# Two slots of one expert run together in a kernel of attention, mixture of experts and GLU

## The chip, the cores and the metric

The kernel runs on one core of a Trainium2 chip. A core has five engines that run their own instruction streams in order and wait for each other by semaphores: TensorE (PE in the profile), VectorE (DVE), ScalarE (ACT), GpSimd (POOL) and SyncE (SP, which here only issues transfers and reads registers). The metric is the device time of one execution in microseconds (us), the time of the slowest core, which is the only one here.

## The reference

Causal attention with a decay bias for 4 batches of 8 heads (576 positions, 64 dimensions) gives 2304 rows `x` of 512 values. Each row goes to one of 8 experts, the one with the largest logit, and the result to a gated linear layer.

```python
def _moe_ref(x, modality_id, w_gate, modality_bias, w1, w2):
    logits = x @ w_gate + modality_bias[modality_id]
    e_idx = np.argmax(logits, axis=1)
    ...
    gate_w = probs[np.arange(N), e_idx]
    for e in range(E):
        mask = e_idx == e
        h = np.maximum(x[mask] @ w1[e], 0.0)
        out[mask] = gate_w[mask, None] * (h @ w2[e])
    return out

def _moe2_ref(x, w_gate, w_val, w_out):
    gate = 1.0 / (1.0 + np.exp(-(x @ w_gate)))
    val = x @ w_val
    return (gate * val @ w_out)
```

## The kernel before

The program is three stages on one hand-written order of instructions; every engine runs its instructions in the order in which the program issues them.

**Attention** works on 16 pairs of heads, four pairs to a batch, by a table of steps that repeats with each pair. Its PE work ends with `trx` and `ptx` (L381), which turn a pair's output into rows of x and its router logits (`lg`). DVE copies them to `xr` and `lg` (L404, L408).

**The router** works on a batch when its four pairs are through. `Router.batch` puts its steps on a list, and `tick`, called at fixed places of the attention's table, takes one of them and then leaves out `GAP[b]` calls; `SP[b]` calls are left out ahead of each scatter. The steps: a chain of ten short DVE instructions (L626 to L632, L655) finds the row's expert; two kinds of small matmuls, `rp` (L639, L641), give each row its rank among the rows of its expert; DVE turns that into an address, `r_ix` (L664); POOL scatters the row's number to a table in DRAM with five indirect DMAs (`tab`, L671); SP stores the rows themselves to `x` in DRAM (`rows_out`, L713). After batch 1 the expert with most rows so far is guessed, its first 512 row numbers are fetched (`idx0`), and SP loads the guessed expert's weights (`on_guess`): four chunks of w1 and w2, 512 KB each, into `raw`.

**The experts** run in slots of 256 rows. The first two slots (EARLY = 2) both belong to the guessed expert and take rows of batches 0 and 1; they start while batches 2 and 3 are still in the router. A slot needs its rows gathered (`gather`, two indirect DMAs on POOL, `xg`, L949), scaled by the gate (`gate`, L962, on POOL), and transposed on PE (`mtr`, L973, eight matmuls, then `xT` on ACT and DVE, L978 and L979). Its work is cut into eight pieces f of 128 hidden units. For each piece the fp32 weights are split into a high and a low part (`split`, tile `ew`: two casts on ACT at L922 and two subtractions on DVE at L925; the first three pieces do both on POOL, L920 and L925). One unit of PE work is `mm1` of a piece (12 matmuls, `ph`, L989) and then `mm2` of the unit before it (12 matmuls, L1009, into `sb` for an even slot, into `y` for an odd one). The 16 units of the first two slots are called u0 to u15 here; slot 0 is u0 to u7, slot 1 is u8 to u15, and each piece is split twice, once for each slot.

`look` (slot 0's transposes) and u0 stand inside the last steps of attention. Then `early` issues u1 to u15. Behind each unit it calls `main`, which takes up to 14 steps from the router's list (`pump`): batch 3's chain, its ranks and scatters, then `slots`, which computes the list of the remaining slots, fetches the 40 table rows that they need from `tab` into `tid` (POOL, L716, which waits until every scatter has landed) and transposes them on PE (`itr`, L725) into `idx`, the addresses for the gathers of slots 2 and on. In program order `itr` stands behind u7. Slot 2's weights are loaded into the same `raw` buffers when their old content has been split for slot 1. The results of a slot go through one buffer `yt` (L1021, two copies on ACT) to DRAM (L1023, SP).

Of the kernel before, what the change touches and what calls it, by code (L numbers as in the profile page):

```python
# [498 lines left out]
TROWS, PUMP = 96, 14  # L499
GAP, SP = [1, 1, 0, 0], [6, 3, 6, 0]  # L500
EARLY, EARLYB, MAIN, SLOTS, FIRST = 2, 2, 9, 14, 3
MAINH, HALVES, HROW, NROW = 2, 8, 32, 40


class Router:
# [102 lines left out]
    def batch(self, b, xr, lg):  # L608

        nc, cp, T = self.nc, self.cp, self.T  # L610
# [3 lines left out]
        tile_ = lambda shape, nm, dt=F32: cp.tile(shape, dt, tag="r_" + nm, name="r_" + nm)  # L614
        st = {}
        self.q.append(lambda: setattr(self, "gap", GAP[b]))
        bc = lambda a: a.unsqueeze(2).to_broadcast([128, 5, 8])
# [7 lines left out]
        q = self.q  # L625
# [42 lines left out]
        for t in range(5):  # L668
            rows = 64 if t == 4 else 128
            self.space(SP[b])  # L670
            q.append(lambda t=t, rows=rows: self.apart("tab", nc.gpsimd.indirect_dma_start(  # L671
                out=self.tab.rearrange("r c -> (r c)").unsqueeze(1),
                out_offset=bass.IndirectOffsetOnAxis(ap=ix[:rows, t : t + 1], axis=0),
                in_=self.ids[:rows, b, t : t + 1], in_offset=None, bounds_check=TROWS * 256 - 1, oob_is_err=True)))
            if t > 2:
                q.append(lambda t=t: self.rows_out(b, t, xr))
        if b == EARLYB - 1:
# [22 lines left out]
            q.append(lambda: V.tensor_copy(self.guess_i, gf[0:1]))  # L700
            q.append(self.on_guess)

    def rows_out(self, b, t, xr):

        x = self.x[2 * self.S * (b // 2) : 2 * self.S * (b // 2 + 1), :].rearrange("(p j) r -> p j r", j=XS)
        if t == 4:
            dst, src = x[64 * (b % 2) : 64 * (b % 2) + 64, 8, :], xr[:64, 4, :]  # L710
        else:
            dst, src = x[:, 4 * (b % 2) : 4 * (b % 2) + 4, :], xr[:, 0:4, :]
        self.nc.sync.dma_start(dst, src)  # L713

    def fetch_rows(self, tid, row, n):
        self.behind("tab", self.nc.gpsimd.indirect_dma_start(  # L716
            out=tid[:n, :], out_offset=None, in_=self.tab[:, :],
            in_offset=bass.IndirectOffsetOnAxis(ap=row[:n, 0:1], axis=0), bounds_check=TROWS - 1, oob_is_err=True,
        ))

    def indices(self, nm, tid, n, last):
# [24 lines left out]
    def slots(self):  # L746
# [5 lines left out]
        nc, T, q = self.nc, self.T, self.q  # L752
# [73 lines left out]
        op(V.scalar_tensor_tensor, out=more, in0=inc[0:1, 8:9], scalar=float(MAIN), in1=s0[0:1], op0=ALU.is_gt, op1=ALU.max)  # L826
        q.append(lambda: self.indices("idx", self.tid, NROW, self.B * self.S - 1))
        op(V.tensor_copy, rg[:, 2:3], base)
# [53 lines left out]
class Moe:  # L882
# [149 lines left out]

    def mm(self, s, f):
        h = self.mm1(s, f)
        if self.prev:
            self.mm2(*self.prev)
        self.prev = (s, f, h)
# [88 lines left out]

    LE, LA = 2, 3

# [12 lines left out]
    def first(self):  # L1141
        for s in range(EARLY):
            self.gather(s)
        for f in range(self.LE + 1):
            self.split(0, f, self.nc.gpsimd)
            if f == 0:
                self.gate(0)
        self.v, self.u = self.LE + 1, 0

    def look(self):  # L1150
        for h in range(2):
            self.transpose(0, h)

    def step(self, u):
        s, f = divmod(u, 8)
        self.mm(s, f)
        if f == 3 and s >= EARLY and s + 2 < MAIN + MAINH:
            self.gather(s + 2 if s + 2 < MAIN else s + 2 - MAIN + HROW)
        if f == 1 and s + 1 < MAIN and s + 1 != EARLY:
            self.gate(s + 1)  # L1160
        if f == 4 and s + 1 == EARLY:
            self.gate(EARLY, True)
        if f in (4, 5) and s + 1 < MAIN:
            self.transpose(s + 1, f - 4)

    def next(self):
        self.step(self.u)
        self.u += 1
# [6 lines left out]
    def early(self, main):  # L1175

        for u in range(8 * EARLY):
            if u == self.u:
                self.next()
            while not self.ready:  # L1180
                self.ready = main(u)
                if u < 8 * EARLY - 5:
                    break
            self.loads()
            for s in range(EARLY, EARLY + 2):
                if self.ready and s not in self.xg and u >= 8 * (EARLY - 2) + 13 * (s - EARLY):
                    self.gather(s)
            self.aheads(self.LE if self.v < 8 * EARLY else self.LA)

# [534 lines left out]
def kernel(ctx, tc, q, k, v, s, modality_id, moe_w_gate, modality_bias, w1, w2, wg, wv, wo, out):  # L1724
    nc = tc.nc
# [9 lines left out]
    with tc.manual_schedule():  # L1735
# [30 lines left out]
        moe = Moe(tc, raw, ps, att.sb, router, w1, w2, x, x2, ids2, ident)  # L1766
# [16 lines left out]
        def main(u):  # L1783
# [8 lines left out]
            if router.q or not phase[0]:  # L1792
                return False
            for s in range(EARLY):
                moe.place(s, 256 * s)
            more.append(nc.values_load(router.more[0:1, 0:1], min_val=0, max_val=1))
# [103 lines left out]
```

## Time and profile before

| | us |
|---|---|
| median of 3 runs | 949.51 |
| lowest and highest of the 3 | 947.5 and 953.03 |
| profiled execution, device time | 945.87 |
| its span, first to last instruction | 944.1 |
| PE busy in the span | 899.6 (95%) |
| DVE, ACT, POOL busy in the span | 710.0, 554.1, 397.2 |

The rows that the prediction reads stand in a section of their own, below. PE's busy time is modelled, and a stretch in which PE has a low granted clock counts as busy; so a look at the start times of neighbouring units tells more than the busy share. "Idle before" and the name behind an arrow tell what ended a wait.

### The profile page before, as it was taken

Reading aid. Unit: us, or ns where it says so; the run is one execution under the profiler, and the core shown is the slowest. Engines: PE = TensorE matmul, PEld = TensorE weight load, DVE = VectorE, ACT = ScalarE, POOL = GpSimd, SP = SyncE. Lnnn points to the kernel's source line nnn. Section 1 sums busy time; section 2 is a strip of 40 time slices with the busy share of each in tenths; the row PEclk is TensorE's granted clock in tenths of the full one; section 3 lists DMA queues with packets and bytes.
Section 4 is the critical chain, followed back from the end, with each engine's and each line's share of the span. In section 5 each row is a group of like instructions: output and inputs, shape, how many; then the busy total and the mean of one; then the engine's idle time right before and its main releaser. Section 6 shows DMA issues by size and latency. Waiting matters only on the chain. (4 is left out here: it accounts for less than half of the span.)

```text
span 944.1 us, 18712 instructions
## 1 busy us (share of the span) xinstructions
PE 899.6 (95%) x6261; PEld 861.0 (91%) x6261; DVE 710.0 (75%) x1583; ACT 554.1 (59%) x1296; POOL 397.2 (42%) x616
## 2 busy tenths in 40 slices
PE   7999999999997999999999899999999999999996
PEld 6899889888887999999998799999999999889996
DVE  6999999999894688867766667767575747878771
ACT  4999899898643665656544455454545344454440
POOL 7988789798742577776630001010000000111111
PEclk8999999999998999999999999999999999999999
DMA  7667559694382355723467322333232308473501
GB/s 173 157 155 161 135 87 128 165 125 145 139 102 69 95 174 180 280 90 90 137 225 242 99 79 95 112 101 120 70 132 76 126 11 296 137 242 111 168 35 44
DMA packets 163903, 125.34 MB, mean 133 GB/s; under 512 B 86737, under 2 KB 147692, under 8 KB 163286
## 3 DMA queue, kind: packets, MB, share of 16 engines
q1 hardware_dynamic: 158790, 113.62, 44.5%
q0 software_dynamic: 3792, 10.14, 3.2%
q8 instruction: 51, 0.84, 0.4%
q14 instruction: 54, 0.44, 0.2%
q10 hardware_dynamic: 1216, 0.30, 0.1%
HBM read 115.95 MB, written 33.23 MB: 158 GB/s over the span
## 5 line engine op out<-in xcount | busy, mean ns | idle before, releaser
L1342 PE MATMUL X<-a,set 128*128 128x384 f32 x864 | 164.7, 338 | 4.8 <-ACTq L1072 3.0
L1342 PEld LDWEIGHTS X<-a,set 128*128 128x128 f32 x864 | 152.4, 188 | 6.6 <-ACTq L1072 3.1
L861 POOL TENSOR_SCALAR dn<-dr 128x256 int8<-128x256 int8 (+1 forms) x60 | 35.2, 588 | 251.3 <-DMA dr<-in_moe_w_gate_dram 96.6
L925 POOL TENSOR_TENSOR w<-raw,w 128x512 fp32r<-128x512 f32 x56 | 79.6, 1431 | 57.2 <-ACT w L922 54.7
L174 POOL TENSOR_SCALAR bias<-cumB,cumT 128x576 f32<-128x576 f32 (+4 forms) x155 | 82.6, 535 | 25.7 <-DVE nm L293 21.3
L1479 POOL DMA_INDIRECT out_dram<-oy,row x18 | 20.0, 1113 | 169.2 <-ACT oy L1503 92.0
L989 PE MATMUL ph<-xT,w 128*128 128x256 f32 x672 | 90.0, 283 | 0.0
L989 PEld LDWEIGHTS ph<-xT,w 128*128 128x128 f32 x672 | 83.6, 188 | 0.0
L1342 PE MATMUL Y<-a,set 128*128 128x384 f32 x432 | 82.0, 338 | 0.0
L302 ACT ACTIVATE P<-P,nm 128x576 f32<-128x576 f32 (+3 forms) x128 | 79.5, 627 | 3.3 <-DVE nm L293 3.2
L337 DVE TENSOR_TENSOR PL<-pt,PH 128x512 fp32r<-128x512 f32 (+1 forms) x128 | 77.0, 629 | 1.9 <-ACT PH L330 1.4
L1342 PEld LDWEIGHTS Y<-a,set 128*128 128x128 f32 x432 | 76.5, 188 | 0.1
L1351 ACT COPY u<-X 128x384 f32<-128x384 f32 x72 | 34.5, 479 | 62.8 <-PE X L1342 62.7
L293 DVE CUSTOM_DVE_ANT_0 P<-sb,bias 128x320 f32<-128x320 f32 (+3 forms) x128 | 67.1, 548 | 2.4 <-PE sb L284 1.9
L330 ACT CAST PH<-pt 128x512 fp32r<-128x512 f32 (+1 forms) x128 | 64.8, 552 | 6.8 <-PE pt L321 5.2
L321 PE MATMUL pt<-ident,P 128*128 128x128 f32 x448 | 64.2, 277 | 3.1 <-DVE PL L337 1.2
L925 DVE TENSOR_TENSOR w<-raw,w 128x512 fp32r<-128x512 f32 x56 | 57.0, 1019 | 11.6 <-ACT w L922 10.8
L922 ACT CAST w<-raw 128x512 fp32r<-128x512 f32 x112 | 63.5, 619 | 0.0
L993 ACT ACTIVATE hH<-ph 128x256 fp32r<-128x256 f32 x72 | 27.7, 384 | 59.7 <-PE ph L989 59.5
L284 PE MATMUL sb<-KT,QH 128*128 128x288 f32 (+3 forms) x192 | 56.3, 317 | 6.6 <-DVE nm L293 4.7
L321 PEld LDWEIGHTS pt<-ident,P 128*128 128x128 f32 x448 | 50.6, 141 | 9.6 <-DVE PL L337 1.9
L1277 ACT CAST hf<-hp 128x768 fp32r<-128x768 f32 x42 | 34.1, 835 | 38.5 <-DVE hp L1279 35.4
(317 smaller groups left out, 2430.9 us busy)
## 6 DMA issues: line engine op xcount, KB each, us to landing
raw<-in_moe_w_dram SPq DMA_DIRECT2D x80, 512.0 KB
h<-sg SPq DMA_DIRECT2D x72, 192.0 KB
cumB<-cum_d SPq DMA_DIRECT2D x32, 288.0 KB
hp<-h SPq DMA_DIRECT2D x24, 384.0 KB
qraw<-in_q_dram SPq DMA_DIRECT2D x58, 128.0 KB
dr<-in_moe_w_out_dram SPq DMA_DIRECT2D x12, 511.6 KB
dr<-in_moe_w_gate_dram SPq DMA_DIRECT2D x24, 255.2 KB
dr<-in_moe_w_val_dram SPq DMA_DIRECT2D x24, 255.2 KB
```

Source lines behind the costliest of these rows:

```text
L174: (nc.vector if n in FILLB else nc.gpsimd).tensor_scalar(res[i][:rows], cumB[:rows, :m], -1.0, self.cumT[:rows, i, n : n + 1], ALU.mult, A ...
L284: nc.tensor.matmul(self.sb[:rows, o : o + c1 - c0], X[:, T0[i] : T0[i] + rows], h["KT"][:, c0:c1], start=j == 0, stop=j == 1)
L293: nc.vector.tensor_tensor_reduce(out=pt[:rows, :m], in0=self.sb[:rows, o : o + m], in1=self.bias_t[n][i][:rows], op0=ALU.add, op1=ALU.min, ...
L302: nc.scalar.activation(h["P"][i][:rows, : T0[i] + rows], h["P"][i][:rows, : T0[i] + rows], AF.Exp, bias=h["nm", i][:rows], scale=-1.0, acc ...
L321: nc.tensor.transpose(pt[:, c : c + 128], h["P"][i][:, T0[j] : T0[j] + 128], self.ident)
L330: self.nc.scalar.copy(t[:, :z], pt[:, :z])
L337: self.nc.vector.tensor_tensor(t[:, :z], pt[:, :z], h["H"][u][:, :z].bitcast(F32), ALU.subtract)
L861: nc.gpsimd.tensor_scalar(o["n"], top(), 56.0, -56.0, ALU.min, ALU.max)
L922: nc.scalar.copy(v, src)
L925: (eng or nc.vector).tensor_tensor(v, src, h.bitcast(F32), ALU.subtract)
L989: nc.tensor.matmul(ph, w[:, 128 * dc : 128 * dc + 128], x[:, dc], start=k == 0, stop=k == 11)
L1342: self.nc.tensor.matmul(bank, w[:, c], a[:, h, c], start=first and k == 0, stop=k == 5, skip_group_check=True)
```

## The change

- **The two slots together.** Units alternate between slot 0 and slot 1 (f, s = divmod(u, 2)), so that both slots use one split of a piece: eight splits where there were sixteen. The first three are on POOL as before, with slot 0's gate behind the first and slot 1's gate behind the second (both on POOL). Slot 1's transposes move from the middle of slot 0 to the start of `early`, ahead of the first `pump`. The loads of slot 2's weights are listed earlier, as each chunk is through after two splits.
- **The table rows.** `itr` and the computation of `idx` come behind u9 (IDX = 9), with the store of the two slots' row numbers (`place`) and slot 2's gather; slot 3's gather behind u13; slot 2's gate behind u12 and its transposes between the two halves of u14 and u15.
- **The router's pace.** GAP goes from [1, 1, 0, 0] to [1, 0, 0, 0] and SP from [6, 3, 6, 0] to [6, 3, 1, 0], so steps of batches 1 and 2 are taken at earlier places of the table. `on_guess` moves from the end of batch 1's list to the head of batch 2's.
- **Batch 3's rows** are stored by DMAs of POOL, behind its five scatters and ahead of the fetch of `tid`, where SP stored them.

```diff
-GAP, SP = [1, 1, 0, 0], [6, 3, 6, 0]
-EARLY, EARLYB, MAIN, SLOTS, FIRST = 2, 2, 9, 14, 3
+GAP, SP = [1, 0, 0, 0], [6, 3, 1, 0]
+EARLY, EARLYB, MAIN, SLOTS, IDX = 2, 2, 9, 14, 9
...
+        if b == EARLYB:
+            self.q.append(self.on_guess)
         self.q.append(lambda: setattr(self, "gap", GAP[b]))
...
-            if t > 2:
-                q.append(lambda t=t: self.rows_out(b, t, xr))
+            if t > 2 and b < self.B - 1:
+                q.append(lambda t=t: self.rows_out(b, t, xr, nc.sync))
+        if b == self.B - 1:
+            for t in (3, 4):
+                q.append(lambda t=t: self.rows_out(b, t, xr, nc.gpsimd))
...
+    def numbers(self):
+        self.indices("idx", self.tid, NROW, self.B * self.S - 1)
...
-        q.append(lambda: self.indices("idx", self.tid, NROW, self.B * self.S - 1))
...
-    def mm(self, s, f):
+    def mm(self, s, f, between=None):
         h = self.mm1(s, f)
+        if between:
+            between()
         if self.prev:
             self.mm2(*self.prev)
...
-        for f in range(self.LE + 1):
+        for f in range(3):
             self.split(0, f, self.nc.gpsimd)
-            if f == 0:
-                self.gate(0)
-        self.v, self.u = self.LE + 1, 0
+            if f < EARLY:
+                self.gate(f)
+        self.e, self.u, self.v = 3, 0, 8 * EARLY
+        self.pend.append((EARLY, 0))
...
+    def both(self, u):
+        f, s = divmod(u, EARLY)
+        self.shared = self.piece[s, f] = self.shared if s else self.piece[s, f]
+        left = 8 * EARLY - u
+        self.mm(s, f, (lambda: self.transpose(EARLY, 2 - left)) if left < 3 else None)
+        if left == 4:
+            self.gate(EARLY, True)
...
     def early(self, main):
+        for h in range(2):
+            self.transpose(1, h)
         for u in range(8 * EARLY):
             if u == self.u:
                 self.next()
             while not self.ready:
                 self.ready = main(u)
-                if u < 8 * EARLY - 5:
+                if u < IDX:
                     break
+            if u == IDX:
+                self.r.numbers()
+                for s in range(EARLY):
+                    self.place(s, 256 * s)
+                self.gather(EARLY)
+            if u == 8 * EARLY - 3:
+                self.gather(EARLY + 1)
+            while self.e < min(8, u // EARLY + 3):
+                self.split(0, self.e)
+                if self.e % 2 == 1:
+                    self.pend.append((EARLY, self.e // 2))
+                self.e += 1
             self.loads()
...
```

The lists of instructions show what this makes of the engines. The names: `vhl` is attention's v, `xg` the gathered rows of a slot (the lower number is slot 0), `ew` a split weight, `tab` a scatter, with `r_ix` of batch 2 (the lower number) or batch 3.

POOL in the last head pair of attention, before:

```order
L202 TENSOR_TENSOR vhl<-vraw_110,vhl 128x10x64
L949 DMA xg_5065<-x,idx_4692 128x513 x2
L949 DMA xg_5066<-x,idx_4692 128x513 x2
L920 TENSOR_SCALAR ew<-raw_0_81 128x512
L925 TENSOR_TENSOR ew<-raw_0_81,ew 128x512
L920 TENSOR_SCALAR ew<-raw_0_82 128x512
L925 TENSOR_TENSOR ew<-raw_0_82,ew 128x512
L962 TENSOR_SCALAR xg_5065<-xg_5065 128x512 x2
```

Gathers, one piece's split, slot 0's gate; batch 2's scatters follow eight rows further down. The same place with the change:

```order
L202 TENSOR_TENSOR vhl<-vraw_110,vhl 128x10x64
L673 DMA tab<-ids,r_ix_4584 24576x1 x5
L955 DMA xg_5091<-x,idx_4391 128x513 x2
L955 DMA xg_5092<-x,idx_4391 128x513 x2
L926 TENSOR_SCALAR ew<-raw_0_81 128x512
L931 TENSOR_TENSOR ew<-raw_0_81,ew 128x512
L926 TENSOR_SCALAR ew<-raw_0_82 128x512
L931 TENSOR_TENSOR ew<-raw_0_82,ew 128x512
L968 TENSOR_SCALAR xg_5091<-xg_5091 128x512 x2
```

Batch 2's five scatters now stand ahead of the gathers, where they stood behind three pieces' splits.

POOL after the third piece's split, before:

```order
L925 TENSOR_TENSOR ew<-raw_1_84,ew 128x512
L671 DMA tab<-ids,r_ix_4578 24576x1 x5
L962 TENSOR_SCALAR xg_5066<-xg_5066 128x512 x2
L671 DMA tab<-ids,r_ix_5265 24576x1 x5
L716 DMA tid<-tab,row 40x256
```

Slot 1's gate and both batches' scatters end here, and the fetch follows. With the change:

```order
L931 TENSOR_TENSOR ew<-raw_1_84,ew 128x512
L673 DMA tab<-ids,r_ix_5284 24576x1 x5
L717 DMA x<-xr_197 128x2052
L717 DMA x<-xr_197 64x513
L720 DMA tid<-tab,row 40x256
```

Slot 1's gate has left this place, and the two stores of batch 3's rows stand between its scatters and the fetch.

PE around batch 3's ranks (`oh` is the one-hot list of experts that DVE makes at the end of its chain), before; the first row is the end of the `mm2` that follows u1's `mm1`:

```order
L1009 MATMUL sb<-hL,ew 128x256
L1009 MATMUL sb<-hH,ew 128x256
L639 LDWEIGHTS tri
L639 MATMUL rp<-oh_193,tri 128x48
L641 LDWEIGHTS ones
L641 MATMUL rp<-oh_193,ones 128x40
```

The ranks follow a whole unit. With the change, from the last rows of attention on:

```order
L381 MATMUL trx<-wgx,oT 128x144 x3
L381 MATMUL ptx<-wgx,oT 128x144 x2
L979 MATMUL mtr<-ident,xg_5092 128x128 x8
L641 LDWEIGHTS tri
L641 MATMUL rp<-oh_193,tri 128x48
L643 LDWEIGHTS ones
L643 MATMUL rp<-oh_193,ones 128x40
```

The ranks now come straight behind slot 1's transposes, where u1's `mm1` and a whole `mm2` stood between them and the last `ptx`.

## Rows read from the trace of the kernel before

**Rows 1.** The page's first part: busy time, share of the span, instructions.

```profile
PE 899.6 (95%) x6261; PEld 861.0 (91%) x6261; DVE 710.0 (75%) x1583; ACT 554.1 (59%) x1296; POOL 397.2 (42%) x616
```

**Rows 2.** Windows of 5 us: busy time by engine, granted clock, DMA share, GB/s.

```profile
260.00:265.00 5.00, 4.87 (x46) 4.76 (x45) 4.29 (x21) 2.54 (x7) 4.04 (x5) 1.00 1.19 131
...
285.00:290.00 5.00, 0.64 (x3) 0.52 (x4) 0.30 (x2) 1.14 (x2) 1.03 (x1) 0.81 0.03 8
290.00:295.00 5.00, 5.00 (x24) 5.00 (x25) 1.72 (x3) 0.38 (x1) 3.47 (x4) 0.51 0.35 96
```

**Rows 3.** Timeline of PE: start, duration, line, operation, tile, count [idle before, releaser].

```profile
253.09 1.12 PE L973 MATMUL mtr<-ident,xg 128*128 128x128 f32 x8
...
259.06 1.69 PE L989 MATMUL ph<-xT,ew 128*128 128x256 f32 x12
...
262.32 0.18 PE L639 MATMUL rp<-oh,tri 128*128 128x48 bf16 x1
...
276.05 1.46 PE L989 MATMUL ph<-xT,ew 128*128 128x256 f32 x10 [0.44 <-DVE ew L925]
...
279.93 1.46 PE L989 MATMUL ph<-xT,ew 128*128 128x256 f32 x10 [0.74 <-DVE ew L925]
...
289.10 0.43 PE L725 MATMUL itr<-ident,tid 40*128 40x40 f32 x2 [6.28 <-DMA tid<-tab,row]
289.80 2.90 PE L989 MATMUL ph<-xT,ew 128*128 128x256 f32 x12 [0.26 <-PE itr L725]
...
295.00 1.60 PE L989 MATMUL ph<-xT,ew 128*128 128x256 f32 x12
...
297.88 1.60 PE L989 MATMUL ph<-xT,ew 128*128 128x256 f32 x12
...
306.57 0.66 PE L973 MATMUL mtr<-ident,xg 128*128 128x128 f32 x4
306.98 1.69 PE L989 MATMUL ph<-xT,ew 128*128 128x256 f32 x12
...
316.14 1.10 PE L989 MATMUL ph<-xT,w 128*128 128x256 f32 x8
```

**Rows 4.** Timeline of POOL, the same columns.

```profile
236.80 1.13 POOL L949 DMA_INDIRECT xg<-x,idx  x1 [0.17 <-issue]
...
241.92 0.62 POOL L920 TENSOR_SCALAR ew<-raw 128x512 fp32r<-128x512 f32 x1
...
245.87 1.37 POOL L962 TENSOR_SCALAR xg<-xg 128x512 f32<-128x512 f32 x2
...
258.26 1.10 POOL L671 DMA_INDIRECT tab<-ids,r_ix  x1 [3.21 <-DVE r_ix L664]
...
264.49 2.38 POOL L962 TENSOR_SCALAR xg<-xg 128x512 f32<-128x512 f32 x2
...
286.54 1.03 POOL L716 DMA_INDIRECT tid<-tab,row  x1 [11.55 <-DMA tab<-ids,r_ix]
```

**Rows 5.** Timeline of DVE, the same columns.

```profile
240.66 1.07 DVE L337 TENSOR_TENSOR PL<-pt,PH 128x320 fp32r<-128x320 f32 x2
...
254.40 1.29 DVE L979 TENSOR_TENSOR xT<-mtr,xT 128x512 fp32r<-128x512 f32 x2 [0.71 <-ACT xT L978]
...
260.17 0.49 DVE L626 TENSOR_REDUCE r_L<-lg 128x40 f32<-128x320 f32 x1
...
262.07 0.19 DVE L632 TENSOR_TENSOR oh<-iotax,r_em 128x40 bf16<-128x40 f32 x1
```

**Rows 6.** DMA issues from 255 to 295 us: engine, count, median us to landing.

```profile
tab<-ids,r_ix POOLq DMA_INDIRECT x10, 14.2
xg<-x,idx POOLq DMA_INDIRECT x4, 4.0
```

**Rows 7.** Timeline of ACT, the same columns.

```profile
295.20 1.08 ACT L1021 COPY yt<-sb 128x512 f32<-128x512 f32 x2 [2.09 <-PE sb L1009]
```

**Rows 8.** View of the tile x: its DMAs, from issue to landing.

```profile
DMA to landing us min/median/max: 3.6/4.2/6.9
```

More of the change, by code (lines that the diff above doesn't have):

```diff
@@ L700, in batch, with rows_out @@
             q.append(lambda: V.tensor_copy(self.guess_i, gf[0:1]))
-            q.append(self.on_guess)
-    def rows_out(self, b, t, xr):
+    def rows_out(self, b, t, xr, eng):
         x = self.x[2 * self.S * (b // 2) : 2 * self.S * (b // 2 + 1), :].rearrange("(p j) r -> p j r", j=XS)
@@ L712, in rows_out @@
             dst, src = x[:, 4 * (b % 2) : 4 * (b % 2) + 4, :], xr[:, 0:4, :]
-        self.nc.sync.dma_start(dst, src)
+        eng.dma_start(dst, src)
     def fetch_rows(self, tid, row, n):
@@ L1125, in half_end @@
         self.hprev = None
-    LE, LA = 2, 3
+    LA = 3
     def ahead(self, v):
@@ L1158, in step @@
             self.gather(s + 2 if s + 2 < MAIN else s + 2 - MAIN + HROW)
-        if f == 1 and s + 1 < MAIN and s + 1 != EARLY:
+        if f == 1 and s + 1 < MAIN:
             self.gate(s + 1)
-        if f == 4 and s + 1 == EARLY:
-            self.gate(EARLY, True)
         if f in (4, 5) and s + 1 < MAIN:
@@ L1166, in next @@
     def next(self):
-        self.step(self.u)
+        (self.both if self.u < 8 * EARLY else self.step)(self.u)
         self.u += 1
@@ L1181, in early @@
                 self.ready = main(u)
-                if u < 8 * EARLY - 5:
+                if u < IDX:
                     break
+            if u == IDX:
[10 more added lines that the diff above has]
+                self.e += 1
             self.loads()
[L1185 to L1188, printed above, removed]
+            if self.e == 8:
+                self.aheads(self.LA)
     def run(self, step):
@@ L1793, in main @@
                 return False
-            for s in range(EARLY):
-                moe.place(s, 256 * s)
             more.append(nc.values_load(router.more[0:1, 0:1], min_val=0, max_val=1))
```

## The prediction

> **What bounds the kernel now.** I read the page first: PE is busy for 95% of the span [rows 1], so a change pays only where PE waits or runs slowly, or where it gives PE less to do. Then the windows around the first two slots: from 285 to 290 us PE is busy for 0.64 of 5 us, and from 290 to 295 us its granted clock is 0.51, the lower of its two levels (1.2 for 2.4 GHz) [rows 2]. PE's timeline names the wait: `itr` waits 6.28 us for the table rows `tid`, and the unit that starts at 289.80 takes 5.20 us to the start of the next, where an undisturbed one (295.00 to 297.88) takes 2.88 [rows 3]. That is 2.32 us lost to the clock after the wait. Two further waits of 0.44 and 0.74 us are for a split weight on DVE [rows 3]. POOL's timeline shows why `tid` is late: the fetch stood at 286.54, 11.55 us behind its last scatter, until all scatters had landed [rows 4]; a scatter takes 14.2 us to land in this stretch, a gather 4.0 [rows 6]. So the stretch that the change concerns runs from `look` (253.09) to the first unit with a weight `w` (316.14), 63.05 us [rows 3]; behind it the units follow each other without PE waits, and I take the rest of the program as unchanged.
>
> **The change part by part.** I rebuild this stretch from the rows. From slot 0's transposes to the start of u1 are 5.97 us (253.09 to 259.06), which hold attention's last matmuls, u0's `mm1` and the last `trx` and `ptx`; these stay. Slot 1's transposes behind them take about 1.0 us (eight such matmuls show 1.12, partly overlapped). Then the ranks `rp`, 0.2 us (the first shows 0.18). Fifteen units at 2.88 us are 43.2. Slot 2's two sets of four transposes take 0.4 each (306.57 to 306.98), 0.8 together. `itr` with its small wait is 0.43 and 0.26, 0.7 [all rows 3].
>
> *A new wait ahead of the ranks.* Before, batch 3's DVE chain ran beside u1 and the `mm2` behind it; now nothing stands between slot 1's transposes and `rp`. In the queue of DVE the chain stands behind slot 1's two subtractions. Slot 0's were through at 255.69, 2.6 us after their transposes had begun (253.09); the chain from its first reduction (260.17) to `oh` (262.26) takes 2.1, of which 0.3 is another unit's instruction, so 1.8 [rows 3, 5]. `rp` may start 4.4 us after slot 1's first transpose, and PE is through with them after 0.9: a wait of 3.5. The sum so far is 5.97 + 1.0 + 3.5 + 0.2 + 43.2 + 0.8 + 0.7 = 55.4 us against 63.05: **7.7 us less**. In it are the 6.28 of `itr`, the 2.32 of the clock and the 1.2 of the two waits for weights; I take them as gone, since half the splits are left (a piece every 5.8 us instead of 2.9) and `itr` comes two units later.
>
> *A new wait at `look`.* Slot 0's transposes need its gate, on POOL. Now batch 2's five scatters stand ahead of the gathers, and they need `r_ix`, which now lies behind the VectorE instruction that started at 240.66: about 241.8 with the few short ones between [rows 5]. Five scatters took 258.26 to 264.49, 6.2 us; so the gathers start near 248.3 instead of 236.80. From the first gather to the end of the gate it was 236.80 to 247.24, 10.4 us, with POOL never waiting [rows 4]. That puts the gate's end at 258.7, and PE comes to `look` at 253.09: a wait of 5.6 at least. Behind it stand, on PE, the last `ot` of attention, u0 and all that follows. The other end is set by the landing: if the gathers land only with the scatters issued just ahead of them (14.2 us after a scatter near 247.2, so 261.4 [rows 6]), the gate ends at 262.8 (1.37) or a little later: a wait of 9.7 to 9.9. I take 7.4, between them and nearer to the lower end, because gathers in the trace landed in 4.0.
>
> *The clock behind that wait.* After a wait of 6.28 us the next unit lost 2.32 [rows 3]. A wait of about the same length is new here, but part of the slow stretch would fall into the wait for `oh`, which then hides it. Between 0 and 2.3; I take 1.7.
>
> *One buffer for two results.* Slots 0 and 1 now end one unit apart, and their results share `yt`. The first copy pair started 0.2 us after a unit began and took 1.08 [rows 3, 7]; the transfer out must land, 3.6 to 6.9 us, 4.2 in the middle [rows 8], before ACT may copy again, and it stands in SP's queue behind a weight load. The second pair would be due 2.88 us after the first; it waits 2.4 us or more, and `hH` of the next unit waits behind it on ACT. PE has most of a unit in hand there, since `mm2` follows a unit later. Between 0 and 3.8 us; I take 1.5.
>
> *Without a price.* The eight splits saved (0.62 us a cast on ACT and about as much on DVE) lie beside PE's units. Slot 1's gate, on POOL behind a second split, ends some 6.3 us after slot 0's (4.0 for a split, 241.92 to 245.87, and 2.38), when PE has needed 6.0 to come to slot 1's transposes: even [rows 3, 4]. Batch 3's x rows leave SP's queue, on which only loads for later slots wait. On POOL's queue they stand ahead of the fetch: see below. Slot 2's loads come earlier, and nothing waits for them now.
>
> The sum: −7.7 + 7.4 + 1.7 + 1.5 = **+2.9 us** on the profiled execution, 945.87 to 948.8. The median of the runs shown is 949.51, 3.64 above the profiled one; with that, **952.4**, +0.3%. A measurement of this kernel can tell about 0.5% (4.75 us) from no change, so I call it the same.
>
> **Rivals.** *Faster: no wait at `look`.* If `r_ix` comes early enough, or POOL is so much quicker, that the gate is through by 253.1, the sum is −7.7 + 1.5 = −6.2: 943.3. It would need the gate 5.6 us earlier than the POOL rows allow; for it speaks that with POOL idle DVE's chain runs faster than I assume, and that the ranks may start earlier. With a wait up to about 1.5 and no clock loss it is still over 0.5% faster. Chance 0.16.
>
> *Slower: the gathers land behind the scatters.* All of them go through the software queue, and batch 2's x rows (1 MB, SP) are written at the same time; when that last happened, the DMA engines were fully busy (share 1.19 from 260 to 265 us [rows 2]) and scatters took 14.2 us [rows 6]. With a landing near 263.6 the gate ends at 265, the wait is 11.9, the clock costs its full 2.3: −7.7 + 11.9 + 2.3 + 1.5 = +8.0, 957.5. It decides from a landing of about 261 on, where the sum passes +4.75. The Trainium skill (DMA: Bandwidth & Descriptors, Queues, rings and completion order) says that each pair of a queue row and a DMA engine has one ring whose descriptors are consumed in order, while an engine takes turns between rows packet by packet. By that the gathers would queue behind the scatters in their ring and share the engines with the x store, which is this rival; the gathers of the trace before had no scatter ahead of them, so no row decides it. Chance 0.28.
>
> *Slower: the table rows are late again.* The fetch of `tid` now stands behind batch 3's 1 MB of x on POOL's queue and in the software queue. With u1 at about 269.5, `itr` is due 26.6 us later (nine units, the first `rp` apart); batch 3's scatters start near 270.5, take 6.2 to issue and 14.2 to land, and the fetch 2.5 more (286.54 to 289.10): some 24 us after u1's start. The margin is about 3 us. If the x store holds them up by 4 to 8 us more, +1.5 to +6 on top, say +6.9 in all: 956.4. The Trainium skill (same page, Issuing engines are not separate DMA queues) says that all DMAs share the same 16 engines, whichever engine issues them, so the move to GpSimd gains no bandwidth; no row here separates the two. Chance 0.07.
>
> **How the numbers follow.** Forecast 0.49 (the wait at `look` between 2 and 9), faster rival 0.16, the slower ones 0.35. The likeliest is the forecast, 952.4; its own range is 945 to 957. The range of 8 in 10 goes from the faster rival's time to a little above the slower ones': 943.5 to 959. Chances: faster 0.16, same 0.49, slower 0.35.
>
> **What would show it.** In the profile after: the first scatter of batch 2 near 241.8, gathers near 248, a PE wait of 5.6 to 10 us at `mtr` near 253, released by POOL's gate; a second one of some 3.5 at `rp`; clock 0.5 between them or behind; `itr` without a long wait; ACT waiting at the second `yt` copy; sixteen units of 2.88. It would be wrong if `look` does not wait, if `itr` still does, or if units run slower than 2.88 because DVE or ACT is now late with splits.

## The result, and the profile after

The changed kernel takes 958.9 us in the median of five runs (956.78 to 959.06) against 949.51 of the kernel before in the same job; the ratio is 1.0097 with a 95% interval of 1.0073 to 1.012. It is 1% slower. Of all runs in this document one is far off, one of the ten executions of the first experiment's kernel (3592.17 us); nothing on record says why, and that kernel's ratio leaves it out. The profiled execution of the changed kernel took 956.78 us of device time with a span of 954.8, 10.7 us above the span before.

PE's busy time rose with the span, 907.6 us against 899.6 [rows 1], though PE runs the same number of matmuls. The page's first part, busy time and share, of the changed kernel:

```profile
PE 907.6 (95%) x6261; PEld 868.1 (91%) x6261; DVE 694.8 (73%) x1567; ACT 547.2 (57%) x1280; POOL 396.2 (41%) x618
```

DVE and ACT lost 15 and 7 us of work, 16 instructions each, to the shared splits. PE gained 8 us of "busy" time; by estimate some 7 of them are the low clock, since the mean granted clock of the span fell from 0.991 to 0.984 (0.016 of 954.8 us against 0.009 of 944.1). The windows of the changed kernel (5 us each; busy time of PE, PEld, DVE, ACT and POOL, then granted clock, DMA share and GB/s) show three stretches at the lower level in this part of the program, where the kernel before had one [rows 2]:

```profile
250.00:255.00 5.00, 4.71 (x18) 4.00 (x17) 1.66 (x6) 1.31 (x4) 4.49 (x6) 0.50 1.22 96
...
260.00:265.00 5.00, 4.26 (x14) 3.59 (x15) 2.05 (x5) 1.38 (x3) 4.83 (x6) 0.50 0.13 50
...
275.00:280.00 5.00, 5.00 (x26) 5.00 (x26) 0.96 (x5) 0.38 (x1) 1.70 (x2) 0.52 0.03 7
```

PE's timeline of the changed kernel (start, duration, line, operation, tile, count, idle before and its releaser) answers to [rows 3]:

```profile
260.53 0.48 PE L979 MATMUL mtr<-ident,xg 128*128 128x128 f32 x1 [3.43 <-POOL xg L968]
...
269.20 1.04 PE L979 MATMUL mtr<-ident,xg 128*128 128x128 f32 x8
...
273.59 0.22 PE L641 MATMUL rp<-oh,tri 128*128 128x48 bf16 x1 [3.35 <-DVE oh L634]
...
273.79 2.91 PE L995 MATMUL ph<-xT,ew 128*128 128x256 f32 x12
...
279.06 1.92 PE L995 MATMUL ph<-xT,ew 128*128 128x256 f32 x12
...
294.66 1.67 PE L995 MATMUL ph<-xT,ew 128*128 128x256 f32 x12 [0.72 <-DVE rg L772]
...
303.46 0.31 PE L732 MATMUL itr<-ident,tid 40*128 40x40 f32 x2
...
321.94 1.58 PE L995 MATMUL ph<-xT,w 128*128 128x256 f32 x12
...
330.69 0.38 PE L1015 MATMUL sb<-hH,w 128*128 128x256 f32 x1 [1.47 <-ACT hH L999]
...
339.54 0.60 PE L979 MATMUL mtr<-ident,xg 128*128 128x128 f32 x4
```

`look` begins at 260.53 instead of 253.09, released by the gate on POOL. The ranks wait 3.35 us for `oh`, and the unit behind them (273.79 to 279.06) takes 5.27 us instead of 2.88, at the low clock. `itr` waits for nothing. The first unit with `w` starts at 321.94 instead of 316.14. Behind it PE waits 1.47 us for `hH`, and slot 3's transposes come at 339.54; in the kernel before they came at 330.37:

```profile
330.37 0.60 PE L973 MATMUL mtr<-ident,xg 128*128 128x128 f32 x4
```

POOL's timeline of the changed kernel, which answers to [rows 4], shows why the gate is late:

```profile
240.54 1.10 POOL L673 DMA_INDIRECT tab<-ids,r_ix  x1 [3.58 <-DVE r_ix L666]
...
247.02 1.08 POOL L955 DMA_INDIRECT xg<-x,idx  x1 [0.30 <-issue]
...
252.10 0.63 POOL L926 TENSOR_SCALAR ew<-raw 128x512 fp32r<-128x512 f32 x1
...
259.78 1.37 POOL L968 TENSOR_SCALAR xg<-xg 128x512 f32<-128x512 f32 x2 [3.75 <-DMA xg<-x,idx]
...
291.94 1.09 POOL L720 DMA_INDIRECT tid<-tab,row  x1 [6.54 <-DVE el L772]
```

The five scatters of batch 2 start at 240.54, the gathers at 247.02, and POOL then waits 3.75 us for the gathers to land before it can do the gate. ACT's timeline shows the other new wait, at the second copy into `yt` [rows 7]:

```profile
322.14 1.08 ACT L1027 COPY yt<-sb 128x512 f32<-128x512 f32 x2 [0.85 <-PE sb L1015]
...
328.24 1.07 ACT L1027 COPY yt<-y 128x512 f32<-128x512 f32 x2 [3.70 <-DMA x<-yt]
```

The sum of the prediction beside the two profiled executions, in us:

| part | forecast | measured | from |
|---|---|---|---|
| start of `look` | +7.4 | +7.4 | 253.09 to 260.53 |
| rebuilt stretch without clock | −7.7 | −7.9 | the rest of `look` to `w`: 63.05 before, 61.41 after |
| clock behind `look` and the ranks | +1.7 | +5.4 | 8.67 for 5.97 behind `look`, u1 5.27 for 2.88, u2 3.20 for 2.88 |
| register load behind u6 | 0 | +0.9 | 3.76 us to the unit at 294.66 for 2.88 |
| one `yt` buffer | +1.5 | +3.4 | `w` to slot 3's transposes, 17.60 (321.94 to 339.54) for 14.23 |
| behind that | 0 | +1.5 | to the end of the span: 615.3 us from slot 3's transposes for 613.7 |
| sum | +2.9 | +10.7 | |

### The profile page after: what moved, and what is told of

Its sections match the earlier page's. It is cut to its first block, busy times and chain, and to the rows that moved or that the text cites. A ratio compares the mean times of both kernels' runs of the same rounds, so it can differ in the third digit from the quotient of the medians.

```text
span 954.8 us, 18685 instructions
## 1 busy us (share of the span) xinstructions
PE 907.6 (95%) x6261; PEld 868.1 (91%) x6261; DVE 694.8 (73%) x1567; ACT 547.2 (57%) x1280; POOL 396.2 (41%) x618
## 5 line engine op out<-in xcount | busy, mean ns | idle before, releaser
L174 POOL TENSOR_SCALAR bias<-cumB,cumT 128x576 f32<-128x576 f32 (+4 forms) x155 | 83.1, 538 | 24.6 <-DVE nm L293 20.2
L931 DVE TENSOR_TENSOR w<-raw,w 128x512 fp32r<-128x512 f32 x56 | 53.9, 962 | 17.0 <-ACT w L928 16.1
L360 PE MATMUL ot<-PH,vhl 128*128 128x512 f32 (+3 forms) x160 | 57.1, 366 | 1.4 <-DVE QL L258 1.3
```

The lines of the kernel that those rows point to most:

```text
L174: (nc.vector if n in FILLB else nc.gpsimd).tensor_scalar(res[i][:rows], cumB[:rows, :m], -1.0, self.cumT[:rows, i, n : n + 1], ALU.mult, A ...
L360: nc.tensor.matmul(out[:, q0 : q0 + z - a], w, X[:, a:z], start=k == 0, stop=k == len(mm) - 1, skip_group_check=True)
L931: (eng or nc.vector).tensor_tensor(v, src, h.bitcast(F32), ALU.subtract)
```

## The experiments

**The router's pace undone.** The question was how much of the loss hangs on where batch 2's steps stand.

```diff
-GAP, SP = [1, 0, 0, 0], [6, 3, 1, 0]
+GAP, SP = [1, 1, 0, 0], [6, 3, 6, 0]
```

> The changed kernel with the router's pace of before (GAP and SP undone, nothing else), so that batch 2's scatters and rows come behind the third piece's split again. Theory (batch 2's early scatters and store cost the wait at look, the slow stretch of PE before it and two of the three clock drops): no wait at look, the slot's transposes near 253, the first unit with w near 309 to 311 instead of 321.9, the whole some 10 to 13 us below the changed kernel's 956.8, so 944 to 947, within 0.3% of before. Rival (the loss comes from the rest, the wait for the ranks, the single yt buffer, the store on GpSimd): less than 5 us below the changed kernel, 952 or more.

Measured: 942.24 us against 946.38 of the kernel before in the same job, ratio 0.9957 (0.9935 to 0.9979). The theory held, and the gain was a little larger than expected: the whole of the loss and 0.4% more hang on this one line. It holds two settings that differ, GAP of batch 1 and SP of batch 2, which this run does not tell apart. PE's timeline of this kernel:

```profile
253.19 1.12 PE L979 MATMUL mtr<-ident,xg 128*128 128x128 f32 x8
...
259.32 1.04 PE L979 MATMUL mtr<-ident,xg 128*128 128x128 f32 x8
...
264.19 0.20 PE L641 MATMUL rp<-oh,tri 128*128 128x48 bf16 x1
...
307.05 1.58 PE L995 MATMUL ph<-xT,w 128*128 128x256 f32 x12
```

There is no wait at `look`. There is none at `rp` either, because with the slower pace fewer of the router's steps were done when `early` began: the first call of the router takes 14 steps and does not come as far as the ranks, so u1 runs ahead of them. The stretch from `look` to `w` takes 53.86 us here, 9.2 less than before.

**Two yt buffers in the changed kernel.**

```diff
-        self.yt = self.wk.tile([128, 4, 256], F32, name="yt")
+        self.yts = [self.wk.tile([128, 4, 256], F32, name=f"yt{i}") for i in range(2)]
...
         del self.xg[s]
         y = self.y.pop(s)
+        self.yt = self.yts[s % 2]
```

> The changed kernel with two yt buffers, one for each of two neighbouring slots. Theory (ACT's wait for the first result's transfer sets the units behind u17): the wait of 3.7 us at the second yt copy is gone, units u16 to u21 take 2.85 each, 3.3 to 4.2 us less than the changed kernel: 952.6 to 953.5. Rival (those units are slow because slot 2's weights come or are split late, and the wait only coincides): less than 1 us gained.

Measured: 954.8 us, 1.0088 of before (1.0053 to 1.0122); the gain cannot be told from none, and the 952.6 to 953.5 expected was missed. The trace says why. ACT's second copy into `yt` no longer waits, and the stretch from `w` to slot 3's transposes takes 14.24 us (324.57 to 338.81), 3.4 less. But this execution had lost as much earlier, in attention, where PE's timeline shows a wait that the first profile of the changed kernel did not have:

```profile
216.18 0.39 PE L732 MATMUL itr<-ident,tid 16*128 16x16 f32 x2 [3.91 <-DMA tid<-tab,grow]
...
266.73 0.47 PE L979 MATMUL mtr<-ident,xg 128*128 128x128 f32 x1 [8.02 <-POOL xg L968]
```

The first row is the transposes of the guessed expert's 16 table rows (line L732 of the same helper as `itr`). GAP of batch 1 went from 1 to 0, which brings the transposes from 226.69 to about 211, only 4 us behind the fetch (206.99 to 210.94 in the first profile). In this execution the fetch itself left late, at 212.77: POOL, ahead of it, had waited 3.73 us (to 208.12) for `cumB`, an input of attention's bias, and PE stopped for the fetch. Why that load was late is not known. The second row is the wait at `look` where PE comes undisturbed: 8.0 us.

**The ranks behind u1.**

```diff
-            while not self.ready:
+            while u and not self.ready:
                 self.ready = main(u)
```

> The changed kernel with the first call of the router behind u1 instead of ahead of it, so that batch 3's ranks stand behind a whole unit of PE work as before. Theory (the wait of 3.35 us at rp and the clock drop behind it, 2.4 us, are paid on PE): 5 to 6 us less than the changed kernel, 951 to 952, no clock drop near 273. Rival (the wait only moves, to u1's weights or to the table rows, which are one unit later now): less than 2 us gained, with a wait at u1's first matmul or at itr.

Measured: 955.85 us, 1.0102 (1.0066 to 1.0138), so no gain that can be measured, where 951 to 952 was expected. In this execution too PE waited for the guess's table rows, 2.77 us to 215.4, behind a wait of POOL for `cumB` of 3.13. Where the edit is, it did about what was expected: from slot 1's transposes to u2 are 6.54 us (274.59 to 281.13) instead of 9.86 (269.20 to 279.06), and `rp` still waits 1.35:

```profile
280.97 0.20 PE L641 MATMUL rp<-oh,tri 128*128 128x48 bf16 x1 [1.35 <-DVE oh L634]
```

**Batch 2's store later.** This run did not do what it was meant to.

```diff
-            if t > 2 and b < self.B - 1:
+            if t > 2 and b < self.B - 1 and b != EARLYB:
                 q.append(lambda t=t: self.rows_out(b, t, xr, nc.sync))
+        if b == EARLYB:
+            self.space(24)
+            for t in (3, 4):
+                q.append(lambda t=t: self.rows_out(b, t, xr, nc.sync))
```

> The changed kernel with SP's store of batch 2's rows put 24 places later in the router's list, everything else in place; the scatters stay early. Theory A (the 1 MB store makes the scatters and gathers land late and slows PE's signals to ACT from 244 to 254): PE reaches look near 253, the gather lands within 5 us, slot 0's gate ends near 257 to 258, 3 to 6 us less than the changed kernel: 951 to 954. Theory B (the scatters on GpSimd's queue do it themselves): PE's slow stretch and the landing near 259 stay, within 1.5 us of the changed kernel.

Measured: 956.09 us, 1.0111 (1.0078 to 1.0144). A later place in the list does not hold SP back, which has nothing else to do there: the store went out at 242.98, 1.4 us behind the first scatter, as in the changed kernel. So the run is a repeat of the changed kernel and decides nothing between A and B. As a repeat it shows the wait at `look` again, 8.43 us, with PE there at 253.3.

**Batch 2's scatters later.** On POOL, which is busy there, a later place in the list is a later time.

```diff
+        if b == EARLYB:
+            for t in (3, 4):
+                q.append(lambda t=t: self.rows_out(b, t, xr, nc.sync))
+            self.space(24)
         for t in range(5):
...
-            if t > 2 and b < self.B - 1:
+            if t > 2 and b < self.B - 1 and b != EARLYB:
                 q.append(lambda t=t: self.rows_out(b, t, xr, nc.sync))
```

> The changed kernel with its pace, but batch 2's five scatters put 24 places later in the router's list, so that POOL does them behind the third piece's split; SP's store of batch 2's rows stays early. Theory (the wait at look comes from the scatters ahead of the gathers on POOL and in the software queue, the early store alone does no harm): no wait at look, slot 0's transposes start when PE comes to them, 8 to 13 us less than the changed kernel; what stays is the guess's early transposes, which cost 0 to 6 us near 211 to 216: 942 to 949, 0.996 to 1.003 of before. Rival (the 1 MB store, early, holds the gathers up by itself): a wait of 3 us or more at look, 950 or more.

Measured: 945.52 us against 945.57, ratio 0.9998 (0.9974 to 1.0022). POOL's and PE's timelines:

```profile
237.73 1.13 POOL L959 DMA_INDIRECT xg<-x,idx  x1 [0.16 <-PE ot L360]
...
246.80 1.37 POOL L972 TENSOR_SCALAR xg<-xg 128x512 f32<-128x512 f32 x2
...
257.50 1.10 POOL L677 DMA_INDIRECT tab<-ids,r_ix  x1 [0.16 <-issue]
```

```profile
253.76 1.12 PE L983 MATMUL mtr<-ident,xg 128*128 128x128 f32 x8
...
264.45 0.20 PE L641 MATMUL rp<-oh,tri 128*128 128x48 bf16 x1
...
283.98 2.39 PE L999 MATMUL ph<-xT,ew 128*128 128x256 f32 x12 [1.84 <-DVE rg L776]
```

With the gathers first, the gate is done at 248.2 and `look` does not wait. The place of the scatters in POOL's order is thus worth 1% of the kernel, with all that hangs on it: the ranks come behind u1 here (264.45) and do not wait either, so the wait at `rp` and the low clock behind it are in this 1%.

The run does not clear the store. SP's store goes out as early as in the changed kernel (243.07), but the gathers now leave before it, from 237.73 to 242.8, where in the changed kernel they leave 5 us and more behind it. What the DMA view says of the issues from 236 to 262 us, in the kernel before and then in this run (issues, then the median us to landing of those it can time):

```profile
xg<-x,idx POOLq DMA_INDIRECT x4, 5.7
```

```profile
tab<-ids,r_ix POOLq DMA_INDIRECT x4, 5.8
```

The first row: while weight loads kept the DMA engines busy in the kernel before (370 GB/s), gathers without a scatter ahead landed in 5.7 us. In the three runs of the changed pace above, behind the scatters and the store, they took 11.0 to 11.3. So busy DMA engines alone do not make the 11 us. The second row: without a store beside it, the scatter that the view can time landed in 5.8 us; beside the store they took 14.2 in the kernel before [rows 6] and 13.7 to 14.2 in those three runs. So the store may well be needed for the loss, by way of the scatters. Scatters first without an early store were not run.

The kernel stays 0.4% above the kernel with the whole pace undone, though the intervals touch; in this trace PE waits 1.84 us for the register load behind u6, and the unit behind it takes 4.45 us (to 288.43) at a clock that drops at 284.6.

**The pace undone and two yt buffers.** The edits are those of the first two runs.

> The kernel with the router's pace of before (e1_pace) and two yt buffers. Theory (the single buffer costs PE 3.3 to 4.3 us behind u17): 938 to 939.5 where e1_pace had 942.2, 0.991 to 0.993 of before, no wait of ACT for the transfer of yt. Rival (the gain is given back at the weights of slot 2 or 3): 0.995 to 0.996 of before as e1_pace.

Measured: 938.4 us, 0.9934 (0.991 to 0.9957). From `w` to slot 3's transposes are 14.23 us (305.86 to 320.09), where the same kernel with one buffer takes 17.12 (307.05 to 324.17): 2.9 us less, and as much as in the kernel before (14.23). The theory held. PE's timeline of this kernel:

```profile
305.86 1.58 PE L995 MATMUL ph<-xT,w 128*128 128x256 f32 x12
...
320.09 0.60 PE L979 MATMUL mtr<-ident,xg 128*128 128x128 f32 x4
```

**The register load moved**, from behind u6 to behind u15, in the kernel with the pace undone and two `yt` buffers. It reads the flag `more`, and every engine does it.

```diff
-            more.append(nc.values_load(router.more[0:1, 0:1], min_val=0, max_val=1))
             return True
 
         moe.early(main)
+        more.append(nc.values_load(router.more[0:1, 0:1], min_val=0, max_val=1))
```

> e7_yt with the register load of the flag `more` behind u15 instead of behind u6, where every engine waited for the end of the list of slots. Theory (the wait of 0.77 us on PE in e1_pace at 282.6 and the queue behind it): 0.8 to 1 us less than e7_yt, 0.990 to 0.992 of before. Rival (the engines lose the same at the later place, since the load takes time on each of them): no difference to e7_yt within 0.3 us.

Measured: 937.6 us, 0.9914 (0.9884 to 0.9944). This is the fastest kernel here, called the best kernel below. Its interval and that of the last run overlap, so the gain stands in the trace alone: it has the unit at the old place at 2.88 us (279.54 to 282.42) where it was 3.80 (277.64 to 281.44), 0.9 less. PE's timeline of this kernel around it:

```profile
279.54 1.60 PE L995 MATMUL ph<-xT,ew 128*128 128x256 f32 x12
...
282.42 1.60 PE L995 MATMUL ph<-xT,ew 128*128 128x256 f32 x12
```

**Batch 3's rows stored by SP again**, in the kernel with the pace undone.

```diff
-                q.append(lambda t=t: self.rows_out(b, t, xr, nc.gpsimd))
+                q.append(lambda t=t: self.rows_out(b, t, xr, nc.sync))
```

> e1_pace with batch 3's rows stored by SP again. Theory (that edit is neutral, since the table rows are due two units later): the fetch of tid may come some us later, itr near 288.6 waits for nothing, within 1.5 us of e1_pace, 0.994 to 0.998 of before. Rival (SP's store makes batch 3's scatters land near 285 as before, so that the table rows are late even for the tenth unit): a wait of 1 to 3 us at itr and a clock drop behind it, 2 to 5 us more than e1_pace, 0.998 to 1.001.

Measured: 942.76 us, 0.9972 (0.9957 to 0.9987), which overlaps the 0.9957 of the same kernel with the store on GpSimd. The fetch does come later, 10.6 us behind the last scatter instead of 6.5 (273.18 to 279.69 there). POOL's and PE's timelines with SP's store:

```profile
276.36 1.24 POOL L673 DMA_INDIRECT tab<-ids,r_ix  x1 [3.75 <-DMA tab<-ids,r_ix]
286.98 1.38 POOL L720 DMA_INDIRECT tid<-tab,row  x1 [9.38 <-DVE hL L1000]
```

```profile
290.03 0.31 PE L732 MATMUL itr<-ident,tid 40*128 40x40 f32 x2
```

`itr` at 290.03 waits for nothing even so: the theory held, with little to spare.

**The changed kernel again.**

> The changed kernel once more, beside the others on this chip. Theory: 1.007 to 1.013 of before; the wait at look 8 us where PE comes to it undisturbed (as in e2 to e4), and in some executions a wait of up to 4 us for the guess's table rows near 212, so its executions spread over 5 us or more. Rival (the wait at look is 3.4 us, as in the first profile of the changed kernel): 3 to 4 us at look again.

Measured: 958.15 us against 949.43, ratio 1.0104 (1.0071 to 1.0137). The total is as expected. In the wait the rival was right: in this execution, as in the first profile, PE came to `look` only near 256.6 and waited 3.93 and 1.02 us, once for each half of the gate:

```profile
260.55 0.48 PE L979 MATMUL mtr<-ident,xg 128*128 128x128 f32 x1 [3.93 <-POOL xg L968]
...
262.05 1.76 PE L979 MATMUL mtr<-ident,xg 128*128 128x128 f32 x7 [1.02 <-POOL xg L968]
```

The start of the transposes does not depend on when PE comes: it lies 20.0, 19.8, 19.9, 20.2 and 19.5 us behind batch 2's first scatter in the first profile, the runs with two yt buffers, with the ranks behind u1, with the store meant to be late, and here.

**The best kernel again.**

> e8_more once more, in more rounds (the pace of before, two yt buffers, the flag's register load behind u15). Theory: 0.990 to 0.993 of before, the whole interval below 0.996. Rival: above 0.995, so that its gain in the last job came from the chip.

Measured: 939.47 us against 949.43, ratio 0.99 (0.9876 to 0.9924), as expected. It is faster than the kernel before by 1% and than the changed kernel by 2%.

**Each piece split twice again**, in the best kernel.

```diff
-        for f in range(3):
-            self.split(0, f, self.nc.gpsimd)
...
+        for e in range(3):
+            self.split(e % EARLY, e // EARLY, self.nc.gpsimd)
...
-        self.shared = self.piece[s, f] = self.shared if s else self.piece[s, f]
...
-            while self.e < min(8, u // EARLY + 3):
-                self.split(0, self.e)
...
+            while self.e < min(8 * EARLY, u + 3):
+                f, s = divmod(self.e, EARLY)
+                self.split(s, f)
...
```

> e8_more with every piece of the two slots split twice again, once for each slot, in the order in which the units use them. Theory (the splits saved lie beside PE's units, and only the two short waits for a split weight, 1.2 us in the kernel before, hang on them): 0 to 1.5 us more than e8_more, 0.990 to 0.995 of before. Rival (the shared splits are what carries the gain): waits for ew at several units, 3 us or more, 0.995 to 1.0.

Measured: 943.09 us, 0.9942 (0.9919 to 0.9965), 0.4% above the best kernel. PE's timeline:

```profile
270.82 1.46 PE L995 MATMUL ph<-xT,ew 128*128 128x256 f32 x10 [0.87 <-issue]
...
279.02 1.46 PE L995 MATMUL ph<-xT,ew 128*128 128x256 f32 x10 [1.04 <-DVE ew L931]
...
282.43 1.46 PE L995 MATMUL ph<-xT,ew 128*128 128x256 f32 x10 [0.28 <-DVE ew L931]
```

Units u3 to u6 take 4.0, 4.0, 4.2 and 3.4 us instead of 2.88, where DVE has the router's steps beside the splits (that this is the reason is read from the order, no run shows it). Of the 0 to 1.5 us expected and the 3 or more of the rival, the rival is nearer: the medians of the same job differ by 3.6 us (943.09 for 939.47), and the stretch from `look` to `w` takes 57.91 us for 53.38 in the two traces. The ratio itself still lies in the range that was expected (0.990 to 0.995).

**The table rows' transposes behind u7**, in the best kernel.

```diff
-EARLY, EARLYB, MAIN, SLOTS, IDX = 2, 2, 9, 14, 9
+EARLY, EARLYB, MAIN, SLOTS, IDX = 2, 2, 9, 14, 7
```

> e8_more with the table rows' transposes behind u7 as in the kernel before instead of u9. Theory (batch 3's scatters land some 7 us earlier when its rows are stored behind them on GpSimd's queue, so the fetch leaves near 280 and lands near 283, ahead of u7's end near 285): no wait at itr, within 1 us of e8_more, 0.990 to 0.994. Rival (the two units are needed as well): a wait of 1 us or more at itr, perhaps a clock drop, 0.993 to 0.998.

Measured: 945.14 us, 0.9961 (0.9944 to 0.9978). My expectation fell, the rival was right:

```profile
288.48 0.43 PE L732 MATMUL itr<-ident,tid 40*128 40x40 f32 x2 [3.50 <-DMA tid<-tab,row]
288.84 2.93 PE L995 MATMUL ph<-xT,ew 128*128 128x256 f32 x12
...
294.13 1.81 PE L995 MATMUL ph<-xT,ew 128*128 128x256 f32 x12
```

The fetch left at 284.17 here, not near 280, `itr` waited 3.5 us and the unit behind it took 5.29 at the low clock, 2.4 more than 2.88: 5.9 us together in the trace, and 5.7 between the medians (945.14 for 939.47).

## Why the prediction was right or wrong

The measured 958.9 lies at the upper end of the range, 0.1 us inside it, and the kernel is slower by 1%, where the likeliest case was +0.3% and within the 0.5%. Slower had a chance of 0.35. The mechanism at `look` was right, but the sum of +2.9 us stands against 10.7: the clock and the one `yt` buffer were undersized, and two terms were missing. By its steps:

**The start of `look` held in size, partly by luck.** Forecast was 7.4 us later, 253.09 to 260.5; measured 260.53. The wait itself was 3.43 us in the first profile, where PE came late, and 8.0 to 8.4 where it came undisturbed. The two causes were those of the prediction, but not their shares. It had 5.6 us from POOL's order and some 1.8 from the landing. By POOL's order the gate would have begun at 256.0 and `look` at 256.8, 3.7 us late: the scatters began at 240.54, not near 241.8, and PE starts when the first half of the gate is through, as the two waits in the repeat of the changed kernel show, where the prediction waited for its end. The landing of the gathers added 3.75. The two errors cancelled.

The run with the scatters behind the gathers took the wait away. The second gather of slot 0 was issued at 248.4 and landed near 259.7, 11 us later, where gathers without scatters ahead took 4.0 [rows 6] and 5.7. The Trainium skill (DMA: Bandwidth & Descriptors, Queues, rings and completion order) says that on each DMA engine the descriptors of a ring are consumed in order; by that rule the gathers queue behind the scatters' descriptors, and the trace agrees. It does not prove it: SP's store of 1 MB ran at the same time, and the run that was to take it away did not. How the 3.75 us divide between the two stays open.

**The clock was the step that failed most.** The prediction had one low stretch behind `look`, of which part was hidden, 0 to 2.3, taken as 1.7. There were two that cost: behind `look` (259.29 to 266.12, 2.7 us) and behind the wait for the ranks (272.95 to 279.77, 2.4 us). I had priced the wait of 3.5 us at `rp` rightly (3.35) and not seen that it would cost the clock again. PE waited twice, 13 us apart, and paid the low clock twice. (A third low stretch, 249.05 to 255.88, lay ahead of `look` and cost nothing, since the gate was later still.)

**The `yt` buffer was undersized:** 3.4 us, taken as 1.5 of 0 to 3.8. ACT waited 3.70; the two runs with a second buffer give 3.4 and 2.9 back. In the units behind, `hH` and the splits of slot 2 stand in ACT's queue behind the waiting copy, and PE's lead of a unit was used up: it waited 1.47 us for `hH` at 330.69.

**Two things were missing.** The register load of `more`, 0.9 us, had lain beside the wait for `itr` before (there `more` was ready at 284.4, and PE waited until 289.10); with that wait gone it showed. And the guess's own transposes: the prediction gave GAP of batch 1 no term, but it brings them 16 us forward, to 4 us behind their fetch. In two of the six profiled executions with that pace PE waited there, 2.8 and 3.9 us; in the first profile it did not. The prediction followed the moved steps of batch 2 and not those of batch 1.

**The gain was sized rightly, but not for the reasons given.** The stretch from `look` to `w` without new waits was forecast at 55.4 us with the wait for the ranks, 51.9 without; with the pace undone it is 53.86. The prediction gave the shared splits 1.2 us of it (the two waits for `ew`) and took the rest as cover; split twice, the interleaved order costs 3.6 us. So the shared splits carry more of the gain than the prediction gave them. The later `itr` is worth 5.7 us in the best kernel, which the forecast had as 8.6 (6.28 and 2.32) from the kernel before.

**The rivals.** The slower one named the mechanism and its place; its price of 11.9 us at `look` was too high, and its threshold (a landing from 261 on) too far, because the rest of the sum was too low: with the clock and `yt` as measured, a landing near 259.7 was enough. That its 957.5 is close to the measured time is in part the doing of those other terms. The table rows were not late; the fetch left at 291.94 and `itr` came at 303.46. The faster rival's condition is what the pace undone makes, and it gives 0.9957.

## What to carry to other kernels

A pace setting that moves cheap steps forward moves their DMAs too: before it is made faster, look at what stands behind the moved transfers in the same queue, and who waits for that (here five scatters ahead of four gathers, beside a 1 MB store, delayed PE by 7.4 us, and with what followed cost 1%). Price a new wait on PE with the slow clock behind it, each time it occurs: 3.4 us of waiting at `rp` cost 2.4 more in the next unit. Where work of two slots is interleaved, count every single buffer that the slots share at their end as well as at their start.

## What the runs showed of the hardware that was not expected

- In the first profile ACT was held up while the scatters, the store and the gathers were in flight: its casts at 246.32 and 253.54 were held by something that the profile calls remote, and PE came to `look` near 257 instead of 253. It cost nothing there, since the gate was later still. The rows of ACT in the changed kernel:

```profile
246.32 0.59 ACT L330 CAST PH<-pt 128x512 fp32r<-128x512 f32 x1 [0.88 <-remote]
...
253.54 1.07 ACT L330 CAST PH<-pt 128x512 fp32r<-128x512 f32 x2 [1.93 <-remote]
```

  Its cause stays open: of the four other profiled executions with the early scatters, three came to `look` without it, and the repeat of the changed kernel had it again.
- How long the fetch waits behind the last scatter depends on who stores the rows: 12.5 us before [rows 4] and 10.6 us with SP's store, 6.4 to 8.9 us in the kernels that store them on GpSimd's queue behind the scatters, where the list of slots on DVE is often what the fetch waits for last. The one run that differs by this alone gives 10.6 for 6.5, with no difference in the kernel's time that can be told. By the Trainium skill (DMA: Bandwidth & Descriptors, Issuing engines are not separate DMA queues) all DMAs run on the same 16 engines whoever issues them, so the difference would lie in the order and not in bandwidth; no run here tells the two apart.
